# A twice-folded sequence transform with a paired token order, and mixing steps placed in fixed number

## The chip, the cores and the metric

The kernel runs on one core of a Trainium2 chip. The metric is the device time of one execution in microseconds (us); the number compared is the median of several runs.

## The reference

Two blocks follow each other, all in float32. Attention: batch 4, 8 heads, 768 tokens, 64 values a head, with a block mask (blocks of 32 tokens: neighbours, the first and last block, and three sampled blocks a row). Then a Fourier mix with a channel MLP:

```python
scores = scale * q @ k.T                      # (4, 8, 768, 768)
scores = where(mask, scores, -1e9)
attn = exp(scores - max) / sum;  x = attn @ v # -> (4, 768, 512)
mixed = real(fft(fft(x, axis=1), axis=2))     # over tokens, then over channels
u = x + mixed
un = (u - mean(u)) / sqrt(var(u) + 1e-6)      # over the 512 channels
out = u + relu(un @ w_ch1) @ w_ch2            # 512 -> 2048 -> 512
```

## The kernel before, in words

**Attention.** A token axis of 768 is six tiles of 128 partitions, and all tiles use a token order of the kernel's own (`_ORDER`), in which the partners that the Fourier transform adds and subtracts stand at the same place of two tiles. Tiles 0 to 2 are one half (`xA`), tiles 3 to 5 the other (`xB`). Two heads are a pair, a batch has four pairs, and a pair is cut into six *slots*, 96 in all (24 a batch). A slot computes scores `s` (L573, TensorE), exp (L593 or L601, ScalarE) and values `o` (L647, TensorE). The block mask is added on TensorE at first (`s<-factors`, L583) and later multiplied in on VectorE (L603); `masks["by_pe"]` says which, and it changes over when the first batch's mixing has been placed (`go()` at the end of `begin()`). When a half of a pair is done, its transposed values go through TensorE (`xt`, L670) and one ScalarE copy (L671) into the columns of x.

**Fourier mix of a batch, the *mixing*.** It is a list of steps: the scaling of x by the softmax sums (`norm_steps`, L756); `fold_0`, `fold_1`, `fold_e`, `fold_2` (VectorE: sums and differences of partners, over tokens and over channels); `along(g)` for g = 0 to 3, the transform over tokens (`zp`, TensorE: cosines L827 to L829 for g = 0 and 1, sines L855 for g = 2 and 3, and a small product `side`, L849, for the middle channel); `across(m)`, the transform over channels for each of three tiles (`pq`, and at one tile the extra row `end`); `arrive` (add to x), `spread` (mean and variance on VectorE, the power on GpSimd), `whiten` (VectorE), `un_flip` (`utp`, the transposes, L970), and `right` and `left`, sums for the channel work.

**Channel MLP.** `quad(p)` (L1045) computes one 2x2 block product by seven products (`xp`, `yp`, `z`); `channels()` (L1101) is the second matrix, `y`, four matmuls of 512 columns a tile, added to x on VectorE (L1104); and `store()` (L1112) writes a finished tile of x to `out`, with one DMA for each piece that `_rows` gives. In the last batch `yy` (L1164) does the last products.

**DMAs of a tile.** `_rows(view, tile)` turns the entries of `_ORDER` for a tile into DMAs. An entry is (tile, first partition, runs, jump, length, first token, step). With a positive jump the runs are one DMA with a pattern of [runs, length, row]; with a negative jump each run is a DMA of its own. The tables of cosines and sines and the Q rows of the first part are read through the same function. SyncE's queue issues the loads, the weight chunks and the stores.

**The order of the work.** Python code plans it when the kernel is built. `when` holds planned clocks of the engines, `free` those of the PSUM banks. Channel work waits in `late`, mixing steps in `apart`, short jobs such as `xt` in `short`. `slot(sl)` emits a slot and, between its parts, takes channel steps as owed and calls `gap()`, which places mixing steps whose inputs, by plan, are ready, and places steps that leave a given amount of channel work ahead (`need`). The mixing of batch b begins in the slots of batch b+1, and the channel work of b follows. x has two buffers a half, so the first values of batch b+2 need batch b's stores of that half: `until(finished)` places channel work until the last store of the half has been issued, in slots 53 and 77 (first half, L671 waits for the stores to land) and 55 and 79 (second half). In the last batch everything left is placed without attention beside it.

Of the kernel before, what the change touches and what calls it, by code (L numbers as in the profile page):

```python
# [40 lines left out]
def _grid(ap, start, runs, jump, n, step):  # L41
# [21 lines left out]
_TURNED = (((0, 64, 192, -64, 64, 1), (256, 64, 256, -192, 64, 1), (129, 63, 385, -384, 63, 1),  # L63
            (128, 127, 0, 384, 1, 1), (641, -128, 383, 127, 63, -1), (512, 127, 320, 191, 1, 1)),
           ((384, 64, 191, 64, 64, -1), (704, -128, 64, 63, 63, -1), (640, 127, 0, 1, 1, 1)))

_IN_ORDER = ((0, 129, (256, 127, 2), (64, -128, 2), (1, 2, 64)),  # L70
# [32 lines left out]
def kernel(  # L103
# [19 lines left out]
    P = 128  # L123
# [22 lines left out]
    cs_sb = const.tile([P, T, KS], FP32, name="cs_sb")  # L146
    sn_sb = const.tile([P, T, KS - 1], FP32, name="sn_sb")
# [17 lines left out]
                            op0=ALU.mult)  # L165
    mask = const.tile([P, C, S], U8, name="mask")
# [212 lines left out]
    def table_s(src, dst, t):  # L379
        raw = tr_p.tile([P, ND * HS], FP32, tag="tr", name="tab")  # L380

        def get():
            for p0, cnt, rows in _rows(src, t):
                nc.sync.dma_start(out=raw[p0:p0 + cnt, 0:KS], in_=rows)

        def put():
            to = 0
            for runs, jump, n, s0, step in ODD_EVEN if dst is cs_sb else AS_PLACED:
                nc.vector.tensor_copy(
                    out=dst[:, t, to:to + runs * n].rearrange("p (r n) -> p r n", r=runs),  # L390
                    in_=_grid(raw, s0, runs, jump, n, step))
                to += runs * n
        return get, put

    AS_PLACED = [o[2:] for o in _ORDER if o[0] < T]
    ODD_EVEN = [AS_PLACED[i] for i in (0,)] + [(1, 0, 63, 259, 2), AS_PLACED[3], AS_PLACED[1],
                                               (1, 0, 63, 2, 2), AS_PLACED[4], (1, 0, 1, 384, 1)]

    def table_d(src, dst):
        raw = tr_p.tile([P, ND * HS], FP32, tag="tr", name="tab")  # L400
        row = raw[0:1, KD:2 * KD]

        def get():
            nc.sync.dma_start(out=raw[:, 0:KD], in_=src[0:QD, :])
            nc.sync.dma_start(out=row, in_=src[QD:QD + 1, :])

        def put():
            if dst is cd_sb:
                nc.vector.memset(alt, 0.0)
                for to, frm in ((dst, raw), *((alt[g:g + 1, :], row) for g in (0, 32, 64))):  # L410
# [8 lines left out]
    table_steps = [(table_s, (src, dst, t)) for src, dst in ((cos_s, cs_sb), (sin_s, sn_sb))  # L419
                   for t in range(T)]  # L420
# [70 lines left out]
    def turn(n, a, half):  # L491
# [16 lines left out]
        if a == 1:  # L508
            nc.scalar.copy(out=dst[:, half * HS:(half + 1) * HS], in_=tp[:, 0:HS])
            give(at, busy("ACT", 0.5, done))  # L510
        else:
            for i, (to, to_jump, frm, jump, cnt, step) in enumerate(_TURNED[half]):
                on, copy = (("DVE", nc.vector.tensor_copy) if n == 0 and half == 1
                            else ("ACT", nc.scalar.copy))
                copy(out=_grid(dst, to, 2, to_jump, cnt, 1),
                     in_=_grid(tp, frm, 2, jump, cnt, step))
                end = busy(on, 0.27 if cnt > 1 else 0.18, done)
            give(at, end)
# [249 lines left out]
    def fourier(b, xA, xB, uns):  # L768
# [17 lines left out]
        def fold_e():  # L786

            sa, _, e1 = st["f"]
            b1 = xB[:, 1, :]
# [3 lines left out]
                                           in1=sa[:, 1, 0:M + 1], op0=ALU.mult, op1=ALU.add)  # L793

        def fold_2(i):
# [3 lines left out]
            if i != 1:  # L799
# [9 lines left out]
        folds = [lambda: fold_0(0), lambda: fold_0(1), lambda: fold_1(0), fold_e,  # L809
                 lambda: fold_1(1), lambda: fold_2(0), lambda: fold_2(2), lambda: fold_2(1)]  # L810

        parts = slice(DM - QD, DM), slice(0, QD)

        def along(g):
# [7 lines left out]
            odd = S // 4  # L822

            def cosine(ps, rows, cols):
                mm = nc.tensor.matmul
                for t in (0, 2):
                    mm(ps[rows, 0:KS], sa[:, t, cols], cs_sb[:, t, :], start=(t == 0), stop=False)  # L827
                mm(ps[rows, 0:odd], e1[:, cols], cs_sb[:, 1, 0:odd], start=False, stop=False)
                mm(ps[rows, odd:KS], sa[:, 1, cols], cs_sb[:, 1, odd:KS], start=False, stop=True)  # L829
# [40 lines left out]
        def across(m):  # L870
# [5 lines left out]
            if m == 1:  # L876
# [11 lines left out]
            if m == 1:  # L888
# [4 lines left out]
        def arrive(half, m):  # L893
# [3 lines left out]
            if m == 1 and half == 1:  # L897
# [35 lines left out]
        def d(us, fn, *args):  # L933
# [3 lines left out]
        OPS = {fold_0: 1, fold_1: 1, fold_e: 3, fold_2: 2}  # L937

        first = [d(1.8, fold_0, 0), d(1.8, fold_0, 1), d(1.0, fold_1, 0), d(0.9, fold_e),
                 d(1.0, fold_1, 1), d(1.2, fold_2, 0), d(0.6, fold_2, 2), d(1.3, fold_2, 1)]  # L940
        first += [("mt" if g == 2 else "m", lambda g=g: along(g), 2.1, (1.0 if g < 2 else 0.5), 0.0)
                  for g in range(4)]
        pq = [("m", lambda m=m: across(m), 2.6 if m == 1 else 1.6, 0.7, 0.95) for m in range(T)]
        ar = [[d(1.4 if m == 1 and half == 1 else 1.0, arrive, half, m) for m in range(T)]
# [11 lines left out]
    def mixer(b, xA, xB):  # L956
# [6 lines left out]
        def un_flip(half, m):  # L963
# [3 lines left out]
            tag, pool = (("t", ps_t), ("m", ps_m))[half == 1 and m != 1]  # L967
# [25 lines left out]
        def right(j, *tiles):  # L993
# [8 lines left out]
            def part(ap):  # L1002
                return ap.rearrange("p k (t n) -> p k t n", n=P)[:, :, tiles[0]:tiles[-1] + 1:2, :]
# [146 lines left out]
        def outputs(r, m, after):  # L1150
# [60 lines left out]
            if r == 1:  # L1211
# [3 lines left out]
        fl = [[("tm"[h == 1 and m != 1], lambda h=h, m=m: un_flip(h, m), 0.6, 0.55, 0.0)  # L1215
               for m in range(T)]
              for h in range(2)]
# [138 lines left out]
    def slot(sl):  # L1356
# [103 lines left out]

        must = (3, 5) if paired else (2, 5)
# [157 lines left out]
```

## Time and profile before

| | |
|---|---|
| median of 3 runs | 1062.29 us (1061.76 to 1063.33) |
| span of the profiled execution | 1059.7 us; no other time of that execution is given |
| TensorE busy | 1036.7 us, 4390 instructions |
| VectorE busy | 654.7 us |
| ScalarE busy | 374.3 us |
| GpSimd busy | 235.6 us |
| DMA | 46.65 MB, mean 44 GB/s |
| `y` (L1101) of both halves | 576 passes, 256.6 us |
| `zp` cosine L827, sine L855 | 32 passes, 11.9 us; 48 passes, 17.3 us |
| `side` concurrent products | 0.79 us a batch (830.66 to 831.45 us) |

Times of the profile count from the first instruction, and a matmul in float32 is shown as two passes. Durations of single passes overlap with the next, so the pace is read from the differences of starts. A row of a view gives start, duration, engine, line and operation, what it writes and reads, and shape; an idle time before it and its releaser stand in brackets. A window's row has the window's width, the busy time of each engine, TensorE's granted clock, the DMA engines' busy share and what they moved.

### The profile page before, as it was taken

How to read it: one execution, taken by the hardware profiler on the slowest of the kernel's cores; microseconds unless marked ns; L12 is line 12 of the kernel's file. 1: busy time of each engine (PE TensorE's matmuls, PEld its weight loads, DVE VectorE, ACT ScalarE, POOL GpSimd, SP SyncE). 2: the span in 40 equal slices, each digit the busy share in tenths (PEclk: the TensorE clock that was granted, in tenths of full speed). 3: DMA queues.
4: the chain of work that ended last, by engine and by line, in shares of the span. 5: the costliest groups of instructions: out<-in, count | busy, mean ns of one | idle time of the engine just before them, and what ended most of it. 6: DMA issues, size and time to landing. Idle time of an engine off the chain costs nothing.

```text
span 1059.7 us, 12422 instructions
## 1 busy us (share of the span) xinstructions
PE 1036.7 (98%) x4390; PEld 535.8 (51%) x4390; DVE 654.7 (62%) x1218; ACT 374.3 (35%) x742; POOL 235.6 (22%) x262
## 2 busy tenths in 40 slices
PE   8999999999999999999999999999999999999996
PEld 4333345444455554444444555444445554578575
DVE  6898894667645445664668364765457455575663
ACT  6978855664030112342441302253220211210210
POOL 1000183537000002454553001256520001000000
PEclk9999999999999999999999999999999999999998
DMA  7757422220000002212220001221000001000001
GB/s 214 231 168 232 117 46 45 45 47 15 1 0 1 1 0 48 59 29 54 42 54 2 1 0 30 60 38 28 11 11 6 1 0 32 29 0 1 1 20 43
DMA packets 120803, 46.65 MB, mean 44 GB/s; under 512 B 108176, under 2 KB 113822, under 8 KB 120734
## 3 DMA queue, kind: packets, MB, share of 16 engines
q1 hardware_dynamic: 119484, 45.06, 17.3%
q10 hardware_dynamic: 1218, 0.72, 0.3%
q8 instruction: 36, 0.59, 0.2%
q14 instruction: 33, 0.27, 0.1%
q0 software_dynamic: 32, 0.01, 0.0%
HBM read 37.11 MB, written 6.29 MB: 41 GB/s over the span
## 4 chain that ended last, share of the span: by engine, by line
PE 89%; DVE 4%; DMA 3%; ACT 2%; issue 1%; SPq 0%; POOL 0%; ACTq 0%; DVEq 0%
PE y L1101 23%; PE z L1045 15%; PE s L573 12%; PE o L647 10%; PE yp L1045 7%; PE yy L1164 7%; PE xp L1045 4%; PE zp L855 2%; DMA out_dram<-x 1%; PE s L583 1%; PE zp L827 1%; PE sp L714 1%; PE sp L728 1%; PE utp L970 1%; PE xt L670 1%
## 5 line engine op out<-in xcount | busy, mean ns | idle before, releaser
L633 POOL TENSOR_TENSOR acc<-acc,e 128x384 f32<-128x384 f32 x158 | 159.3, 1042 | 94.1 <-DVE e L603 75.1
L573 PE MATMUL s<-qT,kT 64*128 64x384 f32 x768 | 154.0, 516 | 7.7 <-ACT e L593 4.3
L647 PE MATMUL o<-e,vr 128*64 128x384 f32 x768 | 141.8, 497 | 0.0
L1101 PE MATMUL y<-w_sb,hB 128*128 128x512 f32 x288 | 128.2, 596 | 1.0 <-DVE x L1104 1.0
L1101 PE MATMUL y<-w_sb,hA 128*128 128x512 f32 x288 | 128.4, 595 | 0.0
L603 DVE TENSOR_TENSOR e<-s,mask 128x768 f32<-128x768 f32 x92 | 83.8, 951 | 57.6 <-ACT s L601 47.8
L1104 DVE TENSOR_TENSOR x<-y,x 128x512 f32<-128x512 f32 x72 | 49.7, 690 | 110.9 <-PE y L1101 110.8
L573 PEld LDWEIGHTS s<-qT,kT 64*128 64x128 f32 x768 | 64.2, 186 | 85.8 <-issue 22.1
L601 ACT ACTIVATE s<-s 128x768 f32<-128x768 f32 x92 | 69.9, 792 | 87.5 <-PE s L573 87.0
L1045 PE MATMUL z<-unT,t 128*128 128x384 f32 x256 | 93.1, 486 | 1.2 <-DVE hA L1050 1.2
L633 POOL TENSOR_TENSOR acc<-e 128x384 f32<-128x384 f32 x42 | 47.1, 1142 | 211.6 <-ACT e L593 126.7
L1050 DVE TENSOR_TENSOR hA<-z,hA 128x384 f32<-128x384 f32 x64 | 35.7, 557 | 87.5 <-PE z L1045 87.5
L593 ACT ACTIVATE e<-s 128x768 f32<-128x768 f32 x100 | 76.1, 815 | 36.2 <-PE s L583 31.2
L1101 PEld LDWEIGHTS y<-w_sb,hB 128*128 128x128 f32 x288 | 53.4, 190 | 67.7 <-issue 65.0
L918 POOL TENSOR_SCALAR st<-st 128x1 f32<-128x1 f32 x24 | 8.6, 358 | 346.9 <-DVE st L917 346.8
L1101 PEld LDWEIGHTS y<-w_sb,hA 128*128 128x128 f32 x288 | 53.3, 190 | 62.8 <-issue 59.7
L647 PEld LDWEIGHTS o<-e,vr 128*64 128x64 f32 x768 | 47.9, 136 | 70.3 <-issue 67.9
L1054 ACT ACTIVATE hA<-hA 128x384 f32<-128x384 f32 x64 | 33.5, 523 | 120.3 <-DVE hA L1050 119.9
L1045 PEld LDWEIGHTS z<-unT,t 128*128 128x128 f32 x256 | 48.5, 190 | 35.5 <-DVE hA L1050 2.1
L1054 ACT ACTIVATE hB<-hB 128x384 f32<-128x384 f32 x64 | 33.5, 523 | 86.5 <-DVE hB L1050 84.2
L1065 ACT COPY hA<-xp 128x384 f32<-128x384 f32 x32 | 15.3, 478 | 97.9 <-PE xp L1045 97.9
L1045 PE MATMUL xp<-unT,w_sb 128*128 128x384 f32 x128 | 47.2, 492 | 0.0
(202 smaller groups left out, 1428.7 us busy)
## 6 DMA issues: line engine op xcount, KB each, us to landing
wraw<-in_moe_w_ch_dram SPq DMA_DIRECT2D x32, 512.0 KB
vr<-in_v_dram SPq DMA_DIRECT2D x30, 192.0 KB
qb<-in_q_dram SPq DMA_DIRECT2D x44, 96.0 KB
kb<-in_k_dram SPq DMA_DIRECT2D x44, 96.0 KB
x<-oT SPq DMA_DIRECT2D x192, 12.0 KB
out_dram<-x SPq DMA_DIRECT2D x15, 128.0 KB
out_dram<-x SPq DMA_DIRECT2D x7, 256.0 KB
qr<-in_q_dram SPq DMA_DIRECT2D x24, 64.0 KB
```

The lines of the kernel that those rows point to most:

```text
L573: nc.tensor.matmul(s[:, i, 0:HS], kT[rows, c * P:(c + 1) * P], qT[rows, queries], start=True, stop=u not in by_pe)
L593: nc.scalar.activation(out=e, in_=s[:, :, 0:HS], func=ACT.Exp, scale=scale)
L601: nc.scalar.activation(out=s[:, :, 0:HS], in_=s[:, :, 0:HS], func=ACT.Exp, scale=scale)
L603: nc.vector.tensor_tensor(out=e, in0=s[:, :, 0:HS], in1=m.broadcast_to([P, 2, HS]), op=ALU.mult)
L633: nc.gpsimd.tensor_add(out=acc[:, i, :], in0=start[:, i, :], in1=e[:, i, :])
L647: nc.tensor.matmul(o[D * i:D * i + D, :], vt[:, i, c, :], e[:, i, :], start=(c == 0), stop=(c == C - 1))
L1045: nc.tensor.matmul(to, a[:, k, :], c[:, k, :], start=(k == 0), stop=(k == ND // 2 - 1))
L1050: tt(out=to, in0=ps, in1=a, op=ALU.add)
L1054: nc.scalar.activation(out=h, in_=h, func=ACT.Relu)
L1101: nc.tensor.matmul(y, hs[0, half][:, l, m * P:(m + 1) * P], w2_sb[:, 4 * r + l, :], start=(l == 0), stop=(l == 3))
L1104: nc.vector.tensor_tensor(out=x[:, m, :], in0=y, in1=x[:, m, :], op=ALU.add)
L1164: nc.tensor.matmul(ps, a[:, k, :], c[k // 2][:, k % 2, :] if isinstance(c, list) else c[:, k, :], start=(k == 0), stop=(k == 3))
```

## The change

The token order becomes one of pairs, in which tokens with even and odd numbers stand in the two halves of a tile (`_ORDER`, `_TURNED`, `_IN_ORDER`); the partner of a token for a second fold, over the token axis, then stands at the same partition of another tile. `fold_s` makes this second fold on VectorE, so that the cosine and the sine products use two table tiles instead of three, each with half of the frequencies (odd or even). Two tables of three tiles are now of two. `keep()` writes the results back in the order of frequencies in one or two copies. The extra row `end`, formerly taken at tile 1, is taken at tile 0, and the tiles are mixed in the order 1, 2, 0. Last, `slot()` has a loop: from batch 2's slots on, when no channel work is left and fewer than 18 mixing steps are, it places up to four mixing steps whatever the plan says of their readiness. In the new `_ORDER` the entries with two runs all have a positive jump; before, those of tiles 0 to 2 had a negative one.

```diff
-_ORDER = ((0, 0, 2, -128, 64, 129, 2),
-          (1, 0, 1, 0, 1, 0, 1), (1, 1, 2, -257, 63, 259, 2), (1, 127, 1, 0, 1, 257, 1),
-          (2, 0, 2, -128, 64, 256, 2),
-          (3, 0, 2, 128, 64, 639, -2),
-          (4, 0, 1, 0, 1, 384, 1), (4, 1, 2, 257, 63, 509, -2), (4, 127, 1, 0, 1, 511, 1),
-          (5, 0, 2, 128, 64, 512, -2))
+_ORDER = ((0, 0, 2, 1, 64, 0, 2), (1, 0, 2, 1, 64, 128, 2),
+          (2, 0, 1, 0, 1, 256, 1), (2, 1, 2, 1, 63, 382, -2), (2, 127, 1, 0, 1, 257, 1),
+          (3, 0, 1, 0, 1, 384, 1), (3, 1, 2, 1, 63, 766, -2), (3, 127, 1, 0, 1, 641, 1),
+          (4, 0, 1, 0, 1, 640, 1), (4, 1, 2, 1, 63, 638, -2), (4, 127, 1, 0, 1, 513, 1),
+          (5, 0, 1, 0, 1, 512, 1), (5, 1, 1, 0, 63, 386, 2), (5, 64, 1, 0, 64, 385, 2))
...
-    cs_sb = const.tile([P, T, KS], FP32, name="cs_sb")
-    sn_sb = const.tile([P, T, KS - 1], FP32, name="sn_sb")
+    cs_sb = const.tile([P, 2, KS], FP32, name="cs_sb")
+    sn_sb = const.tile([P, 2, KS - 1], FP32, name="sn_sb")
...
+    not_first = const.tile([P, 2], FP32, name="not_first")
+    nc.vector.tensor_scalar(out=not_first[:, 0:1], in0=first_row, scalar1=-1.0, scalar2=1.0,
+                            op0=ALU.mult, op1=ALU.add)
+    nc.vector.tensor_scalar(out=not_first[:, 1:2], in0=first_row, scalar1=1.0, scalar2=None,
+                            op0=ALU.subtract)
...
+            rows = _rows(src, t)
+            if dst is sn_sb and t == 0:
+                rows = [(0, 1, src[P:P + 1, :]), (1, 63, src[2:P:2, :]), (64, 64, src[1:P:2, :])]
+            for p0, cnt, of in rows:
+                nc.sync.dma_start(out=raw[p0:p0 + cnt, 0:KS], in_=of)
...
+        def fold_s(i):
+
+            def plus(out, tile, by, to):
+                nc.vector.scalar_tensor_tensor(out=out[:, 0:M + 1], in0=tile[:, 0:M + 1], scalar=by,
+                                               in1=to[:, 0:M + 1], op0=ALU.mult, op1=ALU.add)
+
+            sa, sd, e1 = st["f"]
+            if i == 0:
+                plus(e1, sa[:, 2, :], not_first[:, 1:2], e1)
+                plus(sa[:, 0, :], sa[:, 2, :], not_first[:, 0:1], sa[:, 0, :])
+                plus(sa[:, 1, :], sa[:, 2, :], first_row, sa[:, 1, :])
+                plus(sa[:, 2, :], sa[:, 2, :], flip, sa[:, 1, :])
+            else:
+                plus(sd[:, 0, :], sd[:, 0, :], not_first[:, 0:1], sd[:, 2, :])
+                plus(sd[:, 2, :], sd[:, 2, :], -2.0, sd[:, 0, :])
 
...
-            odd = S // 4
-
-            def cosine(ps, rows, cols):
-                mm = nc.tensor.matmul
-                for t in (0, 2):
-                    mm(ps[rows, 0:KS], sa[:, t, cols], cs_sb[:, t, :], start=(t == 0), stop=False)
-                mm(ps[rows, 0:odd], e1[:, cols], cs_sb[:, 1, 0:odd], start=False, stop=False)
-                mm(ps[rows, odd:KS], sa[:, 1, cols], cs_sb[:, 1, odd:KS], start=False, stop=True)
-
-            def keep_cosine(dst, ps):
-                nc.scalar.copy(out=dst, in_=ps[:, 0:KS])
-
-                nc.scalar.copy(out=_grid(dst, P + 1, 2, 63, 63, 1),
-                               in_=_grid(ps, P, 2, 65, 63, 1))
-                nc.scalar.copy(out=_run(dst, P, 2, P - 1), in_=_run(ps, P + 64, 2, -1))
+
+            def odd(ps, rows):
+                return ps[rows, 0:ODD], slice(0, ODD)
+
+            def even(ps, rows, n=ODD):
+                return ps[rows, ODD:ODD + n], slice(ODD, ODD + n)
+
+            def keep(dst, ps, n):
+                nc.scalar.copy(out=_at(dst, 64, [(-64, 2), (P, T), (1, 64)]),
+                               in_=_at(ps, 0, [(ODD, 2), (64, T), (1, 64)]))
+                if n == KS:
+                    nc.scalar.copy(out=dst[:, n - 1:n], in_=ps[:, n - 1:n])
+
+            def product(to, table, *terms):
+                ps, ks = to
+                for t, lhs in enumerate(terms):
+                    nc.tensor.matmul(ps, lhs, table[:, t, ks], start=(t == 0), stop=(t == 1))
 
             if g < 2:
-                cosine(ps, slice(0, P), parts[g])
-                keep_cosine(st["zc"][:, g, :], ps)
+                cols = parts[g]
+                product(odd(ps, slice(0, P)), cs_sb, e1[:, cols], sa[:, 2, cols])
+                product(even(ps, slice(0, P), ODD + 1), cs_sb, sa[:, 0, cols], sa[:, 1, cols])
+                keep(st["zc"][:, g, :], ps, KS)
                 return
             if g == 2:
                 side, at = ps_t.tile([P, 512], FP32, tag="t", name="side"), bank("t")
-                for i, (lhs, t, cols) in enumerate(((sa[:, 0, :], 0, slice(0, KS)),
-                                                    (sa[:, 2, :], 2, slice(0, KS)),
-                                                    (e1, 1, slice(0, odd)),
-                                                    (sa[:, 1, :], 1, slice(odd, KS)))):
-                    g32 = 32 * min(i, 2)
-                    nc.tensor.matmul(side[g32:g32 + 32, cols], lhs[:, QD:QD + 32],
-                                     cs_sb[:, t, cols], start=True, stop=True,
-                                     tile_position=(0, g32))
+                for lhs, t, part in ((e1, 0, odd), (sa[:, 2, :], 1, odd),
+                                     (sa[:, 0, :], 0, even), (sa[:, 1, :], 1, even)):
+                    rows = slice(32 * t, 32 * t + 32)
+                    to, ks = part(side, rows) if part is odd else part(side, rows, ODD + 1)
+                    nc.tensor.matmul(to, lhs[:, QD:QD + 32], cs_sb[:, t, ks], start=True, stop=True,
+                                     tile_position=(0, 32 * t))
                 st["zs"] = room(0, [P, 3, KS], "zs")
+                nc.gpsimd.memset(st["zs"][64:96, 2, :], 0.0)
             zs = st["zs"]
-            for t in range(T):
-                nc.tensor.matmul(ps[:, 0:KS - 1], sd[:, t, parts[g - 2]], sn_sb[:, t, :],
-                                 start=(t == 0), stop=(t == T - 1))
-            nc.scalar.copy(out=zs[:, g - 2, 0:KS - 1], in_=ps[:, 0:KS - 1])
+            cols = parts[g - 2]
+            product(odd(ps, slice(0, P)), sn_sb, sd[:, 0, cols], sd[:, 1, cols])
+            product(even(ps, slice(0, P)), sn_sb, sd[:, 2, cols], sd[:, 1, cols])
+            keep(zs[:, g - 2, :], ps, KS - 1)
             if g == 2:
-                keep_cosine(zs[0:96, 2, :], side[0:96, :])
+                keep(zs[0:64, 2, :], side[0:64, :], KS)
                 give(at, busy("PE", 0.8) + 1.5)
 
...
-        pq = [("m", lambda m=m: across(m), 2.6 if m == 1 else 1.6, 0.7, 0.95) for m in range(T)]
-        ar = [[d(1.4 if m == 1 and half == 1 else 1.0, arrive, half, m) for m in range(T)]
+        pq = [("m", lambda m=m: across(m), 2.6 if m == 0 else 1.6, 0.7, 0.95) for m in range(T)]
+        ar = [[d(1.4 if m == 0 and half == 1 else 1.0, arrive, half, m) for m in range(T)]
...
-        before = first + [pq[0], ar[0][0], ar[1][0], sp[0][0],
-                          pq[2], wh[0][0], ar[0][2], ar[1][2], sp[0][2],
-                          pq[1], wh[0][2], ar[0][1], ar[1][1], sp[0][1], wh[0][1]]
+        before = first + [pq[1], ar[0][1], ar[1][1], sp[0][1],
+                          pq[2], wh[0][1], ar[0][2], ar[1][2], sp[0][2],
+                          pq[0], wh[0][2], ar[0][0], ar[1][0], sp[0][0], wh[0][0]]
         ri = [[("d", lambda i=i, m=m: right(i, *m), 0.0, 0.0, us) for i in (1, 2, 3, 4)]
-              for m, us in (((0, 2), RIGHT), ((1,), COMBINE))]
+              for m, us in (((1, 2), RIGHT), ((0,), COMBINE))]
         le = [("d", lambda i=i: left(0, i), 0.0, 0.0, COMBINE) for i in (1, 3, 4)]
-        after = ([fl[0][0], sp[1][0]] + le +
-                 [fl[0][2], sp[1][2], wh[1][0], fl[0][1], sp[1][1], wh[1][2],
-                  fl[1][0], fl[1][2], wh[1][1]] + ri[0] + [fl[1][1]] + ri[1])
+        after = ([fl[0][1], sp[1][1]] + le +
+                 [fl[0][2], sp[1][2], wh[1][1], fl[0][0], sp[1][0], wh[1][2],
+                  fl[1][1], fl[1][2], wh[1][0]] + ri[0] + [fl[1][0]] + ri[1])
...
+        for _ in range(4 if phase > 1 and not late and len(apart) < 6 * T else 0):
+            if apart and not late:
+                do_apart()
```

More of the change, by code (lines that the diff above doesn't have):

```diff
@@ L165 @@
                             op0=ALU.mult)
+    first_row = ident[:, 0:1]
+    not_first = const.tile([P, 2], FP32, name="not_first")
[3 more added lines that the diff above has]
+                            op0=ALU.subtract)
     mask = const.tile([P, C, S], U8, name="mask")
@@ L382, in get @@
         def get():
-            for p0, cnt, rows in _rows(src, t):
-                nc.sync.dma_start(out=raw[p0:p0 + cnt, 0:KS], in_=rows)
+            rows = _rows(src, t)
[3 more added lines that the diff above has]
+                nc.sync.dma_start(out=raw[p0:p0 + cnt, 0:KS], in_=of)
         def put():
             to = 0
[L388 to L392, printed above, removed]
+            for s0, n, step in FREQUENCIES:
+                if to < dst.shape[2]:
+                    nc.vector.tensor_copy(out=dst[:, t, to:to + n], in_=_run(raw, s0, n, step))
+                to += n
         return get, put
-    AS_PLACED = [o[2:] for o in _ORDER if o[0] < T]
-    ODD_EVEN = [AS_PLACED[i] for i in (0,)] + [(1, 0, 63, 259, 2), AS_PLACED[3], AS_PLACED[1],
-                                               (1, 0, 63, 2, 2), AS_PLACED[4], (1, 0, 1, 384, 1)]
+    ODD = S // 4
+    FREQUENCIES = ((1, 128, 2), (383, 64, -2), (0, 129, 2), (382, 63, -2), (384, 1, 1))
     def table_d(src, dst):
@@ L409, in put @@
                 nc.vector.memset(alt, 0.0)
-                for to, frm in ((dst, raw), *((alt[g:g + 1, :], row) for g in (0, 32, 64))):
+                for to, frm in ((dst, raw), *((alt[g:g + 1, :], row) for g in (0, 32))):
                     nc.vector.tensor_copy(out=to[:, 0:QD + 1], in_=frm[:, 0:KD:2])
@@ L419 @@
     table_steps = [(table_s, (src, dst, t)) for src, dst in ((cos_s, cs_sb), (sin_s, sn_sb))
-                   for t in range(T)]
+                   for t in range(2)]
     table_steps += [(table_d, (cos_d, cd_sb)), (table_d, (sin_d, sd_sb))]
@@ L511, in turn @@
         else:
-            for i, (to, to_jump, frm, jump, cnt, step) in enumerate(_TURNED[half]):
+            for to, frm, *dims in _TURNED[half]:
                 on, copy = (("DVE", nc.vector.tensor_copy) if n == 0 and half == 1
                             else ("ACT", nc.scalar.copy))
-                copy(out=_grid(dst, to, 2, to_jump, cnt, 1),
-                     in_=_grid(tp, frm, 2, jump, cnt, step))
-                end = busy(on, 0.27 if cnt > 1 else 0.18, done)
+                copy(out=_at(dst, to, [(d[0], d[2]) for d in dims]),
+                     in_=_at(tp, frm, [(d[1], d[2]) for d in dims]))
+                end = busy(on, 0.36 if len(dims) > 1 else 0.18, done)
             give(at, end)
@@ L788, in fold_e @@
             sa, _, e1 = st["f"]
-            b1 = xB[:, 1, :]
+            b1 = xB[:, 0, :]
             tt(out=e1[:, 1:M], in0=b1[:, 1:M], in1=_run(b1, DM - 1, M - 1, -1), op=ALU.add)
@@ L875, in across @@
             across_p(ps, slice(0, P), ks)
-            if m == 1:
+            if m == 0:
                 end = ps_t.tile([P, 512], FP32, tag="t", name="end")
@@ L896, in arrive @@
             x = (xA, xB)[half][:, m, :]
-            if m == 1 and half == 1:
+            if m == 0 and half == 1:
                 row = st["zs"][0:1, 0, :]
@@ L966, in un_flip @@
             un = uns.pop((half, m))
-            tag, pool = (("t", ps_t), ("m", ps_m))[half == 1 and m != 1]
+            tag, pool = (("t", ps_t), ("m", ps_m))[half == 1 and m != 0]
             tp = pool.tile([P, ND, P], FP32, tag=tag, name="utp")
@@ L1002, in part @@
             def part(ap):
-                return ap.rearrange("p k (t n) -> p k t n", n=P)[:, :, tiles[0]:tiles[-1] + 1:2, :]
+                return ap.rearrange("p k (t n) -> p k t n", n=P)[:, :, tiles[0]:tiles[-1] + 1, :]
             to, a, c = {1: (t[1], b12, b11), 2: (t[2], b22, t[1]), 3: (b12, b22, b12),
```

21 lines of the change are left out of this document (9 added, 12 removed), and 10 rows, old and new, of tables (_IN_ORDER, _TURNED).

## The prediction

> **What bounds the kernel now.** I read the page first, then the clock, then TensorE's timeline around the removed lines, the chain of waits, SyncE's queue and windows of busy time.
>
> The page says that TensorE is busy nearly all the time:
>
> ```profile
> PE 1036.7 (98%) x4390; PEld 535.8 (51%) x4390; DVE 654.7 (62%) x1218; ACT 374.3 (35%) x742; POOL 235.6 (22%) x262
> ```
>
> So matmul time taken out counts in full, except where something else ends last. The few idle stretches of TensorE over 0.3 us are where the change can matter in another way: 2.56 us at 67.45, 0.58 and 1.32 near 239 and 247, 1.29 at 413.2, 0.91 at 442.0, and about 1 us in all near 893 to 898.
>
> TensorE's timeline, one cosine product of the last batch (start, duration, count of passes; a float32 matmul is two passes, and ends overlap the next start, so I use differences of starts):
>
> ```profile
> 817.61 1.46 PE L827 MATMUL zp<-cs_sb,sa 128*128 128x385 f32 x4
> 818.91 0.49 PE L828 MATMUL zp<-cs_sb,e 128*128 128x192 f32 x2
> 819.23 0.49 PE L829 MATMUL zp<-cs_sb,sa 128*128 128x193 f32 x2
> 819.56 1.45 PE L1045 MATMUL yp<-t,w_sb 128*128 128x384 f32 x4
> ```
>
> Two matmuls of 385 columns take 1.30 us, one of 192 takes 0.32, one of 193 takes 0.33: time goes by columns, also at half width.
>
> The chain of waits, where batch 0's first half (tile xA) is stored so that batch 2's values can take its room:
>
> ```profile
> 408.41 0.70 DVE x L1104
> 409.13 0.47 SPq L1112
> 409.64 2.36 DMA out_dram<-x
> 412.25 0.48 ACT x L671
> 412.73 0.71 ACT s L601
> 413.47 0.97 DVE e L603
> 414.48 1.78 PE s L573 x8
> 428.93 11.62 DMA out_dram<-x
> ```
>
> The copy into x (L671) waits for the store and is ahead of the slot's exps on ScalarE, so exp, mask and the next scores are late with it. In the last line the other half's store takes 11.62 us to land, against 2.36. SyncE's queue issues both sets:
>
> ```profile
> 401.38 8.86 SPq L1112 DMA_DIRECT2D out_dram<-x  x8
> 420.64 8.82 SPq L1112 DMA_DIRECT2D out_dram<-x  x5
> ```
>
> Windows over the first set, the second set and TensorE's gap at 67.45 (after the bounds: width, the engines' busy times, granted clock, DMA share, GB/s):
>
> ```profile
> 67.00:70.00 3.00, 0.62 (x8) 0.00 (x0) 2.15 (x11) 1.94 (x4) 0.00 (x0) 1.00 0.89 353
> 70.50:74.00 3.50, 3.50 (x17) 1.56 (x15) 3.36 (x7) 3.50 (x8) 0.00 (x0) 0.51 0.92 304
> 410.00:412.00 2.00, 2.00 (x14) 0.74 (x14) 0.00 (x0) 0.00 (x0) 0.00 (x0) 1.00 0.75 163
> 422.00:427.00 5.00, 5.00 (x13) 2.28 (x12) 4.95 (x5) 0.00 (x0) 5.00 (x5) 1.00 0.13 38
> ```
>
> Stores whose rows are one run of 64 or 63 go at 163 GB/s over three quarters of 16 engines; those of two runs in one DMA go at 38 GB/s on 0.13 x 16 = 2 engines. And the gap at 67.45 was followed by 3.4 us of half clock; the gaps of 1.3 us were not.
>
> **The change part by part**, against the profiled span of 1059.7 us. The median of the runs is 1062.29, so 2.6 us lie around the span; no separate time of the profiled execution is given.
>
> *Sequence products.* The two cosine groups go from 2x385+192+193 columns to 2x192+2x193, the two sine groups from 3x384 to 4x192: one full matmul less in each of the 4 groups and 4 batches. 16 x 0.645 = **−10.3**. The side product keeps four concurrent matmuls (0.79 us at 830.66 to 831.45 now): 0. The new fold_s adds 6 STT of 128x257 a batch at 0.49 us (row of L792), some 2.9 us of VectorE; with VectorE at 62% they lie beside channel work. What is late then is the mixing itself, below. The copies out of PSUM (2 to 3 of about 0.5 us a group) and one memset on GpSimd a batch hide in the same way; uncovered they would cost those 0.5 us each, 16 times.
>
> *Batch 0's mixing, slots 48 to 53.* The changed order has the PE mask in two more slots: 2 x 0.32 (scores with mask 1.81 us, without 1.49) = +0.65. Forced steps put three transposes (utp) in slot 48, behind whitening that waits for GpSimd's sums of slot 47: +0.8 (0 to 2). The gaps of 0.58 and 1.32, where VectorE was late with hA, go, since the channel work no longer starts there behind x's scaling: −1.9. Sum **−0.4** (−1.5 to +1.5).
>
> *Stores of the first halves, twice* (slots 53 to 55 and 77 to 79). With the new order tiles 0 to 2 are two-run stores, and so share the two engines one after the other. Three such tiles took 440.55 − 420.64 = 19.9 us from first issue to landing in the second halves, 6.4 a tile by bytes (256 KB at 38 to 45 GB/s is 5.8 to 6.9). Let L be the end of the last y of the half. First packets start at L − 6.0 (two periods of y and utp, 3.9 each, before it, and 1.8 for VectorE and issue); at 6.4, 5.8 and 5.4 us (the first tile shares the engines with loads, and I let the next two go faster) they land at L + 11.6. Scores of the second slot can start 2.1 us later (copy 0.48, exp 0.71, mask 0.97, hops), at L + 13.7. What TensorE has to do meanwhile in the changed order is utp 0.43, y of the other half 3.44, utp 0.43, xt 0.42, scores 1.49, two values 2.73 and a gap of 0.5: until L + 9.45. Stall 4.2, against 1.29 in batch 2's place today: +2.9, and +0.5 for the y gap: +3.4. In batch 3's place there is no stall today: +4.4. Sum **+7.8**; with 5 us a tile it is some +3, with 6.9 a tile +14.
>
> *Clock after these stalls.* The nearest row is the 2.56 us gap, followed by 3.4 us at half clock, which is 1.7 us of lost work. Both stalls are longer. 2 x 1.7 = **+3.4** (0 to +5.1, if the last batch's stall counts too). [...]
>
> *Second half of batch 0's room, slot 55.* The transpose xt now comes behind a whole quad, so the store has landed: the 0.91 gap and a longer score go, **−1.1**.
>
> *Batch 2's mixing, slots 79 to 83.* It begins a quad later; quads stand in slots 83 and 85 instead of 79 and 83, and utp x8 and x4 are forced between, at VectorE's pace (scale, statistics 0.68, aggregate 0.18, whiten 0.5 a tile): **+1.0** (0.2 to 3).
>
> *Last batch.* TensorE's timeline there now:
>
> ```profile
> 897.06 0.60 PE L970 MATMUL utp<-ident,un 128*128 128x128 f32 x4
> 898.01 7.13 PE L1101 MATMUL y<-w_sb,hB 128*128 128x512 f32 x16 [0.35 <-DVE x L1104]
> 904.98 0.60 PE L970 MATMUL utp<-ident,un 128*128 128x128 f32 x4
> 905.42 1.46 PE L1045 MATMUL xp<-unT,w_sb 128*128 128x384 f32 x4
> ```
>
> Five of the six utp hide between y's. In the changed order the mixing starts almost two quads later, and five utp stand together behind the last y. From the end of that y VectorE and GpSimd must do x 0.60, statistics 0.62, aggregate 0.15, whiten 0.46, again statistics and aggregate, the power on GpSimd 0.9, and whiten: about 4.3 us, of which 4 x 0.43 are utp. 2.6 idle and 0.45 ahead of z, against 1.0 today: **+2.2** (1 to 3.5).
>
> *Start and end.* 28 instead of 20 mask copies of 0.11 us, and a third table load in three DMAs instead of two ahead of the weight chunk that ends the 2.56 us gap: **+0.7** (−1 to +3). Four table loads instead of six lighten SyncE's queue. [...] The last store is two-run too, in half rows, with packets today ending at 1057.1: 0.
>
> Sum: −10.3 − 0.4 + 7.8 + 3.4 − 1.1 + 1.0 + 2.2 + 0.7 = **+3.3**. Span 1063.0, time 1065.6.
>
> **Rivals.** *Stores land in time* (faster). The stall is there only if a tile takes over 4.4 us: landing after L + 7.3, from a start at L − 6.0. If two-run stores go faster where fewer loads share the queue, the stalls, the clock loss and today's 1.29 go: 3.3 − 7.8 − 3.4 − 0.8 = −8.7, 1053.6; half of it 1059. For: 163 GB/s next to it. Against: 38 GB/s in a window with hardly any load.
>
> *Clock stays at full.* +3.3 − 3.4 = −0.1, 1062.2. [...] Against: 2.56 us.
>
> *Half-width matmuls don't pay.* A pass of 192 columns is 0.16 us, a weight load 0.19 (PEld rows). If loads set the pace, 8 passes x 0.03 x 16 groups = +3.8: 1069.4. It is also the case in which the folds do not shorten the products as they say. Against: 0.32 for the two passes at 818.91, and the transposes, which go at 0.11 a pass though each has a load of 0.14.
>
> **Numbers.** A change of 0.2% (2.1 us) is about what a measurement can tell from none: faster is below 1060.2, slower above 1064.4. The forecast has 0.45, with its own range 1062 to 1069; stores in time, wholly or half, 0.25; full clock 0.18; no pay 0.12. Faster: the 0.25, 0.05 of the full clock and 0.02 of the forecast, 0.32. Same: 0.10 of the full clock and 0.11 of the forecast, 0.21. Slower: 0.32 of the forecast, 0.03 and 0.12: 0.47. The range 1056 to 1070 leaves out the fullest case of the first rival and what lies above the last.
>
> **What would show it.** Cosine groups of 1.30 us instead of 1.95; stores of the first halves landing 11 us after L; gaps of 4 us ahead of the scores in slots 55 and 79, each followed by a clock of 0.5; five utp behind the last y of the last batch with 2 to 3 us between. It is wrong if those gaps are under 2 us, if TensorE's clock stays 1.0 behind them, or if the products lose less than 10 us.

## The result and the profile after

The changed kernel takes 1076.63 us (1075.41 to 1078.14), against 1062.03 us for the kernel before in the same comparison: a ratio of 1.0137, with a 95% interval of 1.0123 to 1.0152. The forecast was 1065.6 with a range of 1056 to 1070: the direction was right, the size was a quarter of the real one. The profiled execution has a span of 1073.9 us and a time of 1075.65, so the span is 14.2 us longer than before.

TensorE did less, and waited more (page of the changed kernel):

```profile
PE 1033.3 (96%) x4414; PEld 539.6 (50%) x4414; DVE 669.5 (62%) x1227; ACT 365.9 (34%) x736; POOL 240.5 (22%) x270
```

Its busy time falls by 3.4 us only, in part since matmuls at half clock are longer (eight of the scores take 2.73 us there, against 1.78 before). The products themselves are as short as forecast; the last batch's first cosine group, TensorE's timeline:

```profile
846.97 0.49 PE L855 MATMUL zp<-cs_sb,e 128*128 128x192 f32 x2
847.29 1.14 PE L855 MATMUL zp<-cs_sb,sa 128*128 128x192 f32 x6
848.27 3.60 PE L1122 MATMUL y<-w_sb,hA 128*128 128x512 f32 x8
```

From 846.97 to 848.27 is 1.30 us, against 1.95 at 817.61 to 819.56 before.

The first half's stores are where the chain of waits now runs, ahead of the scores of slot 55:

```profile
402.96 3.45 PE y L1122 x8
407.48 0.65 SPq L1133
408.18 9.62 DMA out_dram<-x
418.32 0.81 ACT s L605
419.16 0.97 DVE e L607
420.17 2.73 PE s L577 x8
```

The last `y` ends at 406.41. The DMA of 9.62 us is the last of tile 2's three, a single row issued behind the two-run store of 407.48; in its place stood one of 2.36. It lands at 417.80, 11.4 us behind the last `y` (forecast 11.6). The scores then take 2.73 us instead of 1.78, because of the clock (0.53 granted, third window). Windows over the store, the two gaps of TensorE and the stretches behind them (width, busy times, granted clock, DMA share, GB/s):

```profile
401.00:405.00 4.00, 4.00 (x14) 1.96 (x13) 1.91 (x4) 0.59 (x1) 1.11 (x3) 1.00 0.13 37
415.70:420.10 4.40, 0.17 (x2) 0.00 (x0) 0.94 (x2) 2.15 (x4) 0.00 (x0) 1.00 0.36 88
420.20:423.50 3.30, 3.30 (x9) 1.41 (x10) 1.74 (x2) 2.19 (x5) 0.00 (x0) 0.53 0.31 69
668.20:672.70 4.50, 0.17 (x2) 0.00 (x0) 0.91 (x2) 2.12 (x4) 0.00 (x0) 1.00 0.36 89
673.00:676.30 3.30, 3.30 (x9) 1.29 (x8) 1.57 (x2) 2.15 (x5) 0.00 (x0) 0.50 0.34 74
```

Two engines (0.13 of 16) move 37 GB/s; TensorE does next to nothing for 4.4 and 4.5 us (4.2 forecast), and runs at half clock for 3.3 us behind each gap. (Gaps in this text go by the starts of matmuls and their pace, here 4.47 and 4.60; the brackets of a timeline give some 0.2 less, since the ends of matmuls are modelled.)

The end, which the forecast put at nothing, is longer too: from the last matmul's end to the span's end it is 12.0 us (1061.9 to 1073.9), where it was 8.9. The waits of SyncE's queue for earlier stores, first of the changed kernel from 1048 us on, then of the kernel before from 1037 on (in all, times, longest):

```profile
SPq L1133 <- DMA out_dram<-x: 4.2, 2, 3.1
```

```profile
SPq L1112 <- DMA out_dram<-x: 2.1, 1, 2.1
```

In these traces the DMAs of this queue report their end by eight semaphores in turn (55 to 58 DMAs each), and each waits, before it is issued, for the end of the DMA that had its semaphore before. The wait of 3.1 us is for a two-run store of half rows, issued at 1054.2, which ends only at 1066.0. So the last three stores are issued from 1066.1 on, 3.6 us after VectorE's last sum; the kernel before has no such wait behind its last matmul.

In the last batch the forecast's five transposes do stand together (TensorE's timeline, in brackets the idle time ahead):

```profile
911.98 0.66 PE L991 MATMUL utp<-ident,un 128*128 128x128 f32 x4 [0.68 <-ACT unT L992]
912.90 0.66 PE L991 MATMUL utp<-ident,un 128*128 128x128 f32 x4 [0.26 <-DVE un L950]
914.21 0.65 PE L991 MATMUL utp<-ident,un 128*128 128x128 f32 x4 [0.65 <-DVE un L950]
915.59 0.63 PE L991 MATMUL utp<-ident,un 128*128 128x128 f32 x4 [0.73 <-ACT unT L992]
918.99 1.24 PE L1066 MATMUL z<-t,w_sb 128*128 128x384 f32 x3 [0.18 <-DVE t L1028]
```

And two waits came that the forecast had too small or not at all: VectorE's folds in batch 0, and in slot 82 a values matmul that waits for VectorE:

```profile
698.02 1.51 PE L651 MATMUL o<-e,vr 128*64 128x384 f32 x8 [2.18 <-DVE oT L659]
```

VectorE works there on the sums `t` and `unT` (L1028) that the loop placed by number, and its `oT`, which frees the values' PSUM room, comes after them. These sums are also slow: GpSimd adds exps from 694.96 to 697.20, and a sum of 128x256 takes 1.21 us, where it takes 0.42 in the last batch with GpSimd idle (VectorE's timeline, slot 82 and the last batch):

```profile
696.27 1.21 DVE L1028 TENSOR_TENSOR t<-unT,t 128x256 f32<-128x256 f32 x1
697.40 0.57 DVE L659 STREAM_TRANSPOSE oT<-o 128x384 f32<-128x384 f32 x1
918.51 0.42 DVE L1028 TENSOR_TENSOR t<-unT,t 128x256 f32<-128x256 f32 x1
```

### The profile page after: what moved, and what is told of

The parts are those of the page before. It is cut to its first block, busy times and chain, and to the rows that moved or that the text cites. A ratio compares the mean times of both kernels' runs of the same rounds, so it can differ in the third digit from the quotient of the medians.

```text
span 1073.9 us, 12481 instructions
## 1 busy us (share of the span) xinstructions
PE 1033.3 (96%) x4414; PEld 539.6 (50%) x4414; DVE 669.5 (62%) x1227; ACT 365.9 (34%) x736; POOL 240.5 (22%) x270
## 4 chain that ended last, share of the span: by engine, by line
PE 83%; DVE 5%; ACT 3%; DMA 3%; issue 2%; SPq 2%; POOL 0%; ACTq 0%; DVEq 0%
PE y L1122 22%; PE z L1066 15%; PE s L577 11%; PE o L651 9%; PE yp L1066 7%; PE yy L1185 6%; PE xp L1066 3%; PE zp L855 2%; DMA out_dram<-x 2%; PE s L587 1%; PE sp L718 1%; DVE t L1028 1%; SPq L690 1%; ACT e L597 1%; DMA wraw<-in_moe_w_ch_dram 1%
## 5 line engine op out<-in xcount | busy, mean ns | idle before, releaser
L577 PE MATMUL s<-qT,kT 64*128 64x384 f32 x768 | 156.3, 523 | 16.8 <-DVE e L607 10.4
L607 DVE TENSOR_TENSOR e<-s,mask 128x768 f32<-128x768 f32 x88 | 80.1, 950 | 58.2 <-ACT s L605 49.2
L637 POOL TENSOR_TENSOR acc<-e 128x384 f32<-128x384 f32 x46 | 50.4, 1116 | 225.3 <-ACT e L597 127.3
L605 ACT ACTIVATE s<-s 128x768 f32<-128x768 f32 x88 | 66.9, 792 | 92.3 <-PE s L577 92.0
L597 ACT ACTIVATE e<-s 128x768 f32<-128x768 f32 x104 | 79.0, 809 | 48.6 <-PE s L587 35.8
```

Source lines behind the costliest of these rows:

```text
L577: nc.tensor.matmul(s[:, i, 0:HS], kT[rows, c * P:(c + 1) * P], qT[rows, queries], start=True, stop=u not in by_pe)
L597: nc.scalar.activation(out=e, in_=s[:, :, 0:HS], func=ACT.Exp, scale=scale)
L605: nc.scalar.activation(out=s[:, :, 0:HS], in_=s[:, :, 0:HS], func=ACT.Exp, scale=scale)
L607: nc.vector.tensor_tensor(out=e, in0=s[:, :, 0:HS], in1=m.broadcast_to([P, 2, HS]), op=ALU.mult)
L637: nc.gpsimd.tensor_add(out=acc[:, i, :], in0=start[:, i, :], in1=e[:, i, :])
```

## The experiments

Times are medians; the kernel before ran beside each set: 1062.29 (e1 to e4), 1061.78 (e5 to e8), 1061.46 (e9, e10), 1061.69 (e11, e12).

**e1: single-run stores where rows ascend.**

```diff
-        if jump > 0:
+        if jump > 0 and not (split and step > 0):
```

`split` is true for the calls from `store()` alone.

> The changed kernel, with each two-run store of ascending rows issued as two DMAs of one run (tiles 0, 1 and 5's kind; the 2x63 stores with descending rows stay as they are). Theory S (the stores of two runs, on two DMA engines, are the cost): the gaps of 4.47 and 4.60 us ahead of the scores of slots 55 and 79 fall below 1 us, the two spells of half clock behind them go, and part of the 3.1 us that the end takes longer: 3.2 + 4.5 + 3.4 + about 1 = 12 us less, about 1064.5. Rival M (the mixing comes too late, through the folds and the steps placed by number; TensorE would then wait for something else at the same places): at most 4 us less, over 1072.

Measured: 1066.39, 10.2 us below the changed kernel, ratio to before 1.0041 (1.0026 to 1.0056). The gaps fell to 2.36 and 2.15 us, not under 1, because tile 2 still has a two-run store; the end took 8.6 us instead of 12.0. Theory S stands: stores alone account for most of the loss. The clock is instructive (the two gaps, each with the stretch behind it):

```profile
415.80:418.10 2.30, 0.16 (x2) 0.00 (x0) 0.97 (x2) 2.18 (x4) 0.00 (x0) 0.99 0.36 88
418.20:421.60 3.40, 3.40 (x9) 1.58 (x10) 1.69 (x2) 2.08 (x5) 0.00 (x0) 0.52 0.33 71
666.10:668.20 2.10, 0.16 (x2) 0.00 (x0) 0.97 (x2) 2.10 (x4) 0.00 (x0) 1.00 0.38 92
668.30:671.70 3.40, 3.40 (x12) 1.41 (x13) 2.42 (x3) 2.40 (x5) 0.00 (x0) 1.00 0.36 77
```

Of two nearly equal gaps one is followed by half clock, the other is not.

**e2: without the loop** of four steps a slot (the diff's last three lines taken out).

> The changed kernel without the loop that places up to four mixing steps a slot. Theory S: the gaps of 4.5 us stay, as does the half clock; the stretch of slots 48 to 50 gets about 1 us shorter and that of slots 79 to 83 loses the gap of 2.34 us or moves it, in all 0 to 3 us less: 1073.5 to 1076.6. Rival M: the loop is what makes the mixing's transposes wait, so 4 us or more less.

Measured: 1088.8, 12.2 us *above* the changed kernel; both theories missed. Without the loop batch 2's mixing ends too late for its channel work to be released among the slots: by the instruction order slots 80 to 94 then have attention almost alone, and TensorE waits for exps and masks (gaps of 3.50 at 710.4 and 2.34 at 736.5, each with half clock behind). Of the 13.2 us by which the profiled span is longer, 4.7 lie earlier, at a gap ahead of slot 53's scores and in the half clock behind it (shown at e10). So the loop pays for itself: it repairs a lateness of the mixing. That the folds bring this lateness was not tested.

**e3: the kernel before with two-engine stores.**

```diff
+                cut = 62 if cnt in (63, 64) else cnt
...
```

The 1 or 2 rows that are left go in a DMA of their own.

> The kernel before, with each store of 64 or 63 rows cut into one of 62 rows and a rest of 2 or 1; 62 is twice a prime. [...] Rival M, or a store that isn't bound by the count of engines: under 3 us more.

Measured: 1082.84, ratio 1.0191 (1.0174 to 1.0208): 20.6 us above the kernel before, where theory S, with two engines for these stores, had 12 to 16. Windows over a store, and over the stretch of half clock behind the gap of 9.28 us:

```profile
404.00:408.00 4.00, 4.00 (x13) 1.91 (x12) 1.90 (x4) 0.58 (x1) 0.97 (x2) 1.00 0.12 37
417.30:427.50 10.20, 4.76 (x11) 2.01 (x12) 3.74 (x5) 4.68 (x8) 0.00 (x0) 0.50 0.17 33
```

Cutting two rows off each store takes the rate to 37 GB/s on two engines (0.12 of 16), where 64 rows in one run went at 163 GB/s. So a store needs neither two runs nor the new token order to be slow: 62 rows in one run go like the 2 x 64 rows of the changed kernel (37 GB/s, 0.13 of 16). Why these two patterns get two engines, no run shows.

The surplus over theory S is the end. The stalls (8.0 and 4.5 us) and the half clock behind them (2.1 and 1.7 us) come to 16.3 us, near the 12 to 16 of theory S, but from the last matmul's end to the span's end it is 13.5 us instead of 8.9, 4.6 more, which theory S left out as the prediction had. The clock is half for 10.2 us, but that spell began inside the gap: TensorE works for 4.76 us of it.

**e4: without the second fold.** `fold_s` returns at once.

> The changed kernel with the six instructions of the second fold left out in each batch, with the planned order unchanged, so the transform over tokens is of unfolded values and only the time is of interest. If the folds' 2.9 us of VectorE a batch are hidden except in batch 0, where VectorE also has attention work: the gaps of 0.44 and 1.03 us at 163.5 and 169.3 us go, 1.5 to 2.5 us less, 1074 to 1075. Rival M (the folds make the mixing late in every batch): 5 us less or more. If they are hidden in batch 0 too, as predicted: no change.

Measured: 1074.63, 2.0 us less, which is no more than the spread of the runs; the trace has 1.7 us less lost between slots 34 and 36, and no gap less after that. (Its span is 0.6 us longer than the changed kernel's all the same: the start took longer, half clock lasted 6.8 us at slot 55, and it came once more in the last batch.) The folds are hidden except in batch 0, where the prediction hid them too. There they are also longer, and the sums of exps that come behind them hold up the next exp (changed kernel, timelines of VectorE and ScalarE):

```profile
157.45 1.22 DVE L802 SCALAR_TENSOR_TENSOR sa<-sa,not_first 128x257 f32<-128x257 f32 x1
158.59 1.22 DVE L802 SCALAR_TENSOR_TENSOR sa<-sa,ident 128x257 f32<-128x257 f32 x1
159.85 1.11 DVE L802 SCALAR_TENSOR_TENSOR sa<-sa,flip 128x257 f32<-128x257 f32 x1
169.49 0.81 ACT L597 ACTIVATE e<-s 128x768 f32<-128x768 f32 x1 [3.48 <-DVE acc L632]
```

The same instruction takes 0.48 us in the later batches. Here GpSimd is adding exps for 3.28 of the 3.6 us from 157.4 to 161.0. That these additions make the folds longer was not shown: no run takes them away.

**e5: mixing placed earlier**, AHEAD 5.0 instead of 2.2.

> The changed kernel with AHEAD 5.0 instead of 2.2 in the planner: mixing steps on VectorE are placed where its planned clock is up to 5 us past TensorE's, so the last batch's transform begins two quads earlier again, as before the change, and five of its six transposes stand between y's; channel work stands in slots 79 and 83 again. Theory M2 (besides the stores, mixing placed too late costs 2.9 us in slots 81 to 83 and 3.9 in the last batch): 5 to 7 us less than the changed kernel, 1069.5 to 1071.5. Rival (VectorE really is late, so TensorE waits in other places instead): within 2 us of 1076.6.

Measured: 1075.91, 0.7 us less, within the rival's 2 us, though each has a part in it. The 2.9 us of slots 81 to 83 went, as the theory had it, but the last batch got a wait of its own, with half clock behind it:

```profile
813.12 5.40 PE L1122 MATMUL y<-w_sb,hB 128*128 128x512 f32 x8 [3.51 <-DVE x L1125]
```

Steps placed that early make VectorE late with the channel work.

**e6: filler matmuls in the gaps.**

```diff
+        if sl in (2 * SB + 7, 3 * SB + 7):
+            filler = ps_m.tile([P, 512], FP32, tag="m", name="filler")
+            for _ in range(6):
+                nc.tensor.matmul(filler[:, 0:KS - 1], ident, cs_sb[:, 0, 0:KS - 1],
+                                 start=True, stop=True)
```

> The changed kernel with six matmuls of 384 columns, whose result nothing reads, ahead of the scores of slots 55 and 79, where TensorE has a gap of 4.5 us: 3.9 us of work that fills most of the gap. The stall itself stays. Theory (the half clock comes from the idle time): no half clock behind either place, 2 x 1.7 = 3.4 us less, 1073. Rival (it does not hang on the idle time): nothing gained, 1076.6 or up to 1 us more.

Measured: 1074.19, 2.4 us less. With 4 us of useless work in the gaps, the clock stays at full behind them:

```profile
421.80:425.20 3.40, 3.40 (x12) 1.42 (x13) 2.42 (x3) 2.40 (x5) 0.00 (x0) 1.00 0.31 68
673.00:676.30 3.30, 3.30 (x12) 1.40 (x13) 2.32 (x3) 2.39 (x5) 0.00 (x0) 1.00 0.31 68
```

Each stretch behind a gap lost 1.43 us less, so the half clock does come from idleness. The 0.4 us short of 2 x 1.43 is less than the spread of the runs; in the profiled one, which took 1076.08 us, a gap of 2.34 us elsewhere had half clock behind it, which it did not have in the changed kernel.

**e7: e1, and tile 2 first.**

```diff
-                     for half in range(2) for m in range(T)]
+                     for half in range(2) for m in ((2, 0, 1) if half == 0 else range(T))]
...
-            if m == T - 1:
+            if m == (1 if half == 0 and b < B - 1 else T - 1):
                 finished.add((b, half))
```

> As e1 (stores with ascending rows as single runs), and the first half's y come in the order tile 2, 0, 1, so that its one two-engine store starts first and the last two go over 16 engines. Theory S: the gaps of 2.36 and 2.15 us that e1 kept ahead of the scores of slots 55 and 79 fall under 0.5, and the half clock behind the first goes: 1.9 + 1.7 + 1.7 = 5.3 us less than e1, about 1061. Rival M (mixing too late, other waits take the place): within 2 us of e1.

Measured: 1062.12, ratio to before 1.0003 (0.9994 to 1.0012). The stalls at slots 55 and 79 are gone: the chain of waits there is TensorE throughout (65% `y`, 15% scores, 14% values). What the stores cost was worth the whole difference.

**e8: e7 and e5.**

> e7 and e5 together. If stores and late mixing are separate costs, the gains add: about 1061 less 5 to 6, 1055 to 1056, faster than both kernels. If VectorE is the limit behind the late mixing, 1060 or more.

Measured: 1059.34, ratio 0.9982 (0.9973 to 0.9991). The gain of e5 is added, but so is its wait in the last batch, so 3 to 4 us less than hoped.

**e9: AHEAD 5.0 among the slots, 3.0 in the last batch.**

> e8 with AHEAD 5.0 while there is attention and 3.0 in the last batch. There the transform begins one quad later than in e8, and all six transposes but the last have a y behind them. e8 waits 3.49 us for VectorE at 793.8 in the last batch and has half clock behind it. If that wait is the price of placing VectorE's steps too early, it goes, and no wait of the transposes comes back: 3.5 + 1.7 us and about 1 of the small gaps less, 1053 to 1055. If VectorE is the limit in the last batch whatever the order: 1057 or more.

Measured: 1055.52, ratio 0.9939 (0.9925 to 0.9952), just above what was expected: faster than both kernels. The wait of 3.49 us is down to 0.86 and 1.25 (`y` and `yp`, for VectorE), with full clock.

**e10: e9 without the loop.**

> e9 without the loop that places mixing steps by number. If the loop only makes up for channel work that the planner of the changed kernel did not release in time (e2 without it lost 12 us), AHEAD 5.0 does the same and the loop can go: within 2 us of e9, with the three transposes of slot 48 apart again (up to 1 us less), or up to 1 us more for masked slots. If the loop does something of its own: 5 us or more above e9.

Measured: 1058.49, 3.0 us above e9, between the two cases. With AHEAD 5.0 the loop's 12 us are not needed, since the channel work is released in time; but a gap of 3.50 us opens at 246.3, ahead of slot 53's scores, since VectorE is busy without a break there; so the loop still does something in batch 0. e2 has the very same gap at 246.5. Windows over the gap and behind it, first e10, then e2:

```profile
246.20:249.80 3.60, 0.27 (x4) 0.04 (x2) 3.56 (x8) 0.00 (x0) 0.00 (x0) 1.00 0.01 2
249.80:253.00 3.20, 3.20 (x13) 1.56 (x14) 3.20 (x4) 2.21 (x3) 3.15 (x4) 1.00 0.00 0
```

```profile
246.40:250.00 3.60, 0.27 (x4) 0.02 (x2) 3.56 (x8) 0.00 (x0) 0.00 (x0) 0.82 0.01 2
250.00:253.00 3.00, 3.00 (x9) 1.27 (x9) 2.64 (x3) 0.83 (x2) 2.93 (x4) 0.50 0.00 0
```

The same gap, 0.2 us later in the execution, has full clock behind it in the one and half clock in the other, from 248.7, still inside the gap, until 255.5.

**e11: the kernel before with one term less a product.**

```diff
-                for t in (0, 2):
+                for t in (0,):
...
-            for t in range(T):
+            for t in range(2):
```

> The kernel before without the third table's term of the cosine groups (one matmul of 385 columns) and of the sine groups (one of 384), four a batch; the transform is of two thirds of the tokens' terms, and only the time is of interest. The planner's prices stay, so the order stays. If TensorE's time counts in full where the transform stands: 16 x 0.645 = 10.3 us less, 1051 to 1052.5. If something else ends last there (VectorE's folds, copies): under 7 us less, over 1055.

Measured: 1051.96, 9.7 us less, ratio 0.9904 (0.9889 to 0.9920). TensorE's time counts in full where the transform stands.

**e12: e9 with tables in single runs.**

> e9 with the table loads in single runs too, three loads of [2, 64] rows as six of 64. If two-run table loads hold up the weight chunks behind them in the first 120 us (the term of 0.7 us at the start, or the rule that they use two engines, with 5 us each): 1 to 3 us less than e9, 1052.5 to 1054.5. If not: within 1 us of e9's 1055.5, or 1 us more for the three further issues on SyncE's queue.

Measured: 1053.57, ratio 0.9924 (0.9911 to 0.9938), the fastest version. It is 1.9 us below e9, though the two intervals overlap. In the profiled runs e9 has a gap of 2.04 us at 80.0 and half clock from 83 to 87, e12 has neither; but e10, with e9's tables, has no such gap either. The loads themselves are clear: in e9 the three two-run loads landed 7.8 to 8.8 us after their issue, in e12 their single runs after 2.3 to 4.9. In the trace of the changed kernel, which has e9's loads, they landed after 7.5 to 9.4 us; from the first packet of a load to the last it was 4.5 to 5.4 us, at 36 to 44 GB/s, with two engines busy on them. That they cost the kernel 1 to 2 us is likely, not settled.

## Why the prediction was right or wrong

I added up the matmuls between landmarks (the first scores of a slot, the first `yy`) at their pace, and took the rest as lost. Against the sum of the prediction this gives, in us:

| step | forecast | measured |
|---|---|---|
| sequence products | −10.3 | −10.3 (e11: −9.7) |
| batch 0, slots 34 to 53 | −0.4 | +1.7 |
| stores of the first halves | +7.8 | +8.4 |
| half clock behind them | +3.4 | +2.9 |
| second half, from slot 55 | −1.1 | +0.3 |
| batch 2, from slot 79 | +1.0 | +3.1 |
| last batch | +2.2 | +3.7 |
| start | +0.7 | +1.3 |
| end | 0 | +3.1 |
| sum | +3.3 | +14.2 (span: +14.2) |

All that the prediction named as a sign of its being right was there: groups of 1.30 us, stores landing 11 us behind the last `y`, gaps of over 4 us with half clock behind each, five transposes with waits between them. What failed lies in terms put at nothing or too small.

*Right, by mechanism and by size:* the products, the two stalls of 4.2 us (4.47 and 4.60 in the trace) and the clock behind them. e1, e3, e6 and e11 show each by itself. The rival that put the stores in time is refuted by the 37 GB/s, and the rival of half-width matmuls by the 1.30 us.

*Wrong: the step "the last store is two-run too ...: 0".* I priced the last store alone. What decides is that its issue waits for stores ahead of it, and these had become two-engine stores; e1, which splits some of those, gets the 3.4 us back, and e3, which brings two-engine stores to the kernel before, makes its end 4.6 us longer. The same cost was priced at two places and overlooked at the third.

*Wrong: batch 0.* The step that laid the folds "beside channel work" is true for three batches of four. In batch 0 attention is beside them, VectorE sets the pace, the folds take 1.1 to 1.2 us while GpSimd adds exps, and the exps come later, since they wait for VectorE's sums behind the folds (3.48 us of ScalarE ahead of 169.49): e4 gives 1.7 us in the trace. The gaps of 0.58 and 1.32 did go, as forecast.

*Mis-sized: batch 2.* I priced the scaling, statistics and whitening of the forced transposes, not the sums (`right`, L1028) that the loop also places, and that take 1.21 us beside GpSimd's additions instead of 0.42: they hold up `oT`, for 2.34 us. e5, in whose order they stand elsewhere, loses 2.9 us less there. *Mis-sized: the last batch*, 3.7 instead of 2.2 (the term's own figures, 2.6 + 0.45 − 1.0, give 2.05): the chain through VectorE, GpSimd and ScalarE's copy `unT` waits four times, not once, and z waits for the sums behind the last copy. *Slot 55*: the gap of 0.91 went as forecast, but gaps of 0.41 and 0.63 at 431 and 435 took its place, with 0.3 us more before slot 78. *Start*: the first scores began between 7.9 and 9.3 us in the profiled runs of all kernels, so most of this term is spread from run to run.

The five largest errors, 1.4 to 3.1 us, are all on the same side. Three terms (batch 0, batch 2, last batch) lie slightly above the bounds given for them (1.5, 3 and 3.5), and the end had no bounds at all. The range was not made from these bounds: their upper ends (1.5, 14 for the stores, 5.1 for the clock, 3, 3.5 and 3) with −10.3 and −1.1 add up to +18.7, a time of 1081, but it was closed at 1070, just above the last rival's 1069.4.

On the clock the prediction's row held: all ten gaps of over 4 us in the profiled runs had half clock behind them. For shorter gaps the row is no rule: a gap of 2.36 us (e1) was enough, as that of 2.56 us in the kernel before had been, but a gap of 3.50 us was followed by half clock in e2 and not in e10.

## What to carry to other kernels

An edit of a layout also edits the DMAs that read and write it: compare the rate of each with the old one's (here 163 GB/s for 64 rows in one run, 37 for 2 x 64 rows and for 62), and follow a slow store to all who wait for it, the later DMAs of its queue and the end of the program included. A saving on a bound engine is real and is read from its rows (e11: 9.7 us of the 10.3 that they give); what it costs is in the steps that other engines take over, and each of these has to be priced in the stage where it has the least cover. If idle time of TensorE halves its clock, count it 1.4 to 2.4 us dearer (e6: 1.43; e3: 2.1 and 1.7; e2 at slot 53: 2.4).

## What the runs showed of the hardware that was not expected

The half clock is not set by the length of a gap alone: it came behind gaps of 2.04 (e9), 2.36 (e1), 3.50 (e2) and all ten over 4 us, and not behind others of 2.34 (the changed kernel, at 695.7) and 3.50 us (e10). In e4 it came, from 915.3 to 918.7, behind four gaps of 0.4 to 0.9 us among the transposes of the last batch; the same four gaps had full clock behind them in the changed kernel. A spell of it lasted 3.4 us, 6.8 (e2, 248.7 to 255.5) or 10.2 (e3, 417.3 to 427.5), and the long ones began before their gap had ended. A store of 62 rows ran on two engines at 37 GB/s, where stores of 64 rows had run at 163 GB/s and those of 63 rows at 170 (406.5 to 407.5 us of the kernel before). A fold of 128x257 took 0.48 us alone and up to 1.22 beside GpSimd's additions, a sum of 128x256 0.42 alone and 1.21 beside them.
